# A fused attention and MoE kernel: another order of its loads, with one batch's transposes and one block's sums done in another way

## The chip, the cores and the metric

The kernel runs on one core of a Trainium2 chip. The metric is the device time of one execution in microseconds (us), the median of 10 runs: 512.66 us before the change, all runs between 512.37 and 512.99.

A core has five engines with a queue of instructions each: TensorE (PE) for matmuls and transposes, VectorE (DVE) and ScalarE (ACT) for elementwise work, GpSimd (POOL) and SyncE (SP), which here issue DMAs. [...]Loads are issued by POOL[...]; stores and DMA transposes are issued by SP. An engine runs its queue in order, so an instruction that waits holds up everything behind it.

## The reference

Linformer attention for 8 batches of 8 heads, 1024 positions, head size 64, with keys and values projected to 64 rows; then an MLP with a sigmoid GELU over all 8192 tokens.

```python
k_proj = np.einsum('ks,bhsd->bhkd', E, k)
v_proj = np.einsum('ks,bhsd->bhkd', F, v)
scores = np.matmul(q, k_proj.transpose(0, 1, 3, 2)) / sqrt(64)
attn = softmax(scores)
x = matmul(attn, v_proj)      # (8, 8, 1024, 64) -> tokens x 512
h = x @ w_in                  # 512 -> 2048
g = h * (1.0 / (1.0 + np.exp(-1.702 * h)))
out = g @ w_out               # 2048 -> 512
```

The softmax's maximum is not subtracted by the kernel; the scores are small.

## The kernel before

**Blocks.** The 8192 tokens are cut into 16 blocks `j` of 512; a batch `b` is two blocks, `h = 2b` and `2b + 1`. A block's MLP is 16 calls of `ffn1` (slots 0 to 15, each four matmuls of 128x512 and a GELU on ACT), then `ffn2`, eight parts of eight matmuls (slots `O` = 16 onward; two parts for each of four output tiles of 128 tokens). Block 0 is cut smaller, since its inputs are still arriving: its `ffn1` runs in halves of 256 tokens (slots 0 to 31), and its `ffn2` slots are counted from `Q` = 32.

**Attention between the MLP's slots.** The attention of later blocks is put between the slots by hand: `at(j, slot, f)` files `f`, and `filled(j, slot)` runs it after that slot. TensorE's order is thus fixed by this list. For a batch: `proj(b)` projects `k` and `v` (16 matmuls in pairs, key rows in the lower and value rows in the upper half of PSUM's partitions); `kv_out(b)` copies them out on DVE and, from batch 2 on, transposes `k` by a DMA on SP's queue into `kts[b % 2]`; for batch 1 `k_tr` does it with four TensorE transposes. `q_dma(b)` transposes `q` on SP's queue into `qT[b]`. For a block: `scores(h, u)` for `u` = 0, 1 makes the scores of four heads by two groups of eight small matmuls (`eight`, L262) and their exponentials on ACT (L278).

**Three ways to normalize.** Blocks 0 to 2 use `tok` and `x_tr`: the values with a column of ones, tokens on the partitions, a division, and a transpose back. Block 3 uses `norm`: the sums of the exponentials by eight matmuls with ones, spread over all partitions at once, then DVE's reciprocal of the full 128x512 tile four times. Blocks from 4 on use `sums` (eight matmuls of one row each, two reciprocals), `spread` (the reciprocals are written to DRAM and read back, repeated over 64 partitions, as `rbc`) and `values` (matmuls, then one DVE multiplication by `rbc`).

**PSUM.** `f_tile` takes a bank from the pool `ps_f`, which `ffn1`, `ffn2`, `proj` and the scores share; `x_ps` tiles come from `ps_x`, used by `tok`, `x_tr`, `sums`, `norm`, `values`.

**Loads.** `k_sb`, `v_sb` and `q_sb` are one buffer each (`ldpool` has `bufs=1`), and batch 0's `q` has its own, `q0_sb`. A load waits until the batch ahead has been read. POOL's order at the start is: `k` of batch 0, its `q` in the first two of eight column groups `j`, `v`, the next two `j`, six of eight parts of `w_in`, the second half of `q` in one DMA (Block 1's `q`), two parts of `w_in`, four parts of `w_out`, then `load(1)`: `k`, `v`, `q`. `load(b)` for `b` > 1 is `k`, `q`, `v`. A batch's `q` is eight DMAs of 128 KB, in which each head's row of 64 numbers is a run of its own; `k` and `v` are 1 MB each in longer runs. (Sizes are those in bfloat16.) Each load on POOL's queue also waits for the load eight places ahead of it[...].

**Block 1's `q`** is transposed by TensorE (`q_tr(2)`, `q_tr(3)`, L244, 32 transposes) in slots 20 and 23 of block 0.

**The end.** The last of the 64 output tiles is cut into two halves of 256 columns (L397): ACT copies one, DVE the other (L399), each with its own store.

Of the kernel before, what the change touches and what calls it, by code (L numbers as in the profile page):

```python
# [9 lines left out]
F32 = mybir.dt.float32  # L10
# [7 lines left out]
def kernel(ctx, tc, q, k, v, E, F,  # L18
# [37 lines left out]
        for h, n in [(h, hs) for h in range(0, H, hs)] if isinstance(hs, int) else hs:  # L56
            nc.gpsimd.dma_start(out=dst[b][:, h:h + n, js:js + jn], in_=sv[:, h:h + n, js:js + jn])  # L57

    def load_q(b):
        qt[b] = ldpool.tile([P, J, H, D], BF16, name="q_sb")  # L60
        qv = q[b].rearrange("h (p j) d -> p j h d", p=P)
        for j in range(J):
            nc.gpsimd.dma_start(out=qt[b][:, j], in_=qv[:, j])  # L63

    def load(b):
        load_kv(k, kt, b, "k_sb")
        if b == 1:
            load_kv(v, vt, b, "v_sb")
        load_q(b)
        if b > 1:  # L70
            load_kv(v, vt, b, "v_sb")

    w_in_v = moe_w_in.rearrange("(c p) f -> p c f", p=P)
    w_out_v = moe_w_out.rearrange("(c p) m -> p c m", p=P)
# [8 lines left out]
    load_kv(k, kt, 0, "k_sb", ((0, 4), (4, 2), (6, 2)))  # L83
    ident = consts.tile([P, P], BF16)
    make_identity(nc, ident)
    load_kv(q, qt, 0, "q0_sb", H, 0, 2)
    load_kv(v, vt, 0, "v_sb", ((0, 4), (4, 2), (6, 2)))
    load_kv(q, qt, 0, "q0_sb", H, 2, 2)
    for i in range(6):
        load_w_in(i)  # L90
    load_kv(q, qt, 0, "q0_sb", H, JB, JB)
    for i in range(6, 8):
        load_w_in(i)
    for i in range(4):
        sl = slice(i * FC // 4, (i + 1) * FC // 4)
        nc.gpsimd.dma_start(out=w_out_sb[:, sl, :], in_=w_out_v[:, sl, :])
    load(1)
# [31 lines left out]
    def f_tile(shape, dt=F32):  # L129
        return ps_f.tile(shape, dt, name="f_ps")  # L130
# [24 lines left out]
        return efts[j // (J // 2)][:, j % (J // 2), cols]  # L155


    kvps, kbs, qT, expT, xT, rbc, rdens = {}, {}, {}, {}, {}, {}, {}

    def proj(b):  # L160
        def go():
# [15 lines left out]
    def k_piece(h0, n):  # L177
        k_ps = proj0(0, h0, n)
        k_b = att.tile([KP, n, D], BF16, name=f"k0_b{h0}", bufs=1)
        nc.vector.tensor_copy(k_b, k_ps[LO])  # L180
        warm(2)
        k_tr(0, k_b, h0 // 2)

    def k_tr(b, k_b, p0):
        n = k_b.shape[1] // 2
        t_ps = f_tile([P, n, KP], BF16)
        for p in range(n):
            nc.tensor.transpose(t_ps[:, p, :], k_b[:, 2 * p:2 * p + 2, :].rearrange("k t d -> k (t d)"),
                                ident[:KP, :KP])
        nc.vector.tensor_copy(kts[b % 2][:, p0:p0 + n, :], t_ps)  # L190

    def vx_of(b, p):
        if b == 1:
# [21 lines left out]
    def kv_out(b):  # L215
        def go():
            ps = kvps.pop(b)
            k_b = att.tile([KP, H, D], BF16, name="k_b")
            nc.vector.tensor_copy(k_b, ps[LO])  # L219
            if b > 1:  # L220
                nc.sync.dma_start_transpose(out=kts[b % 2], in_=k_b.rearrange("k h d -> k (h d)"))
            v_out(b, ps)
            kbs[b] = k_b
        return go

    q0s = [[consts.tile([P, 2, 2, P], BF16, name=f"q0T{g}{u}") for u in range(2)] for g in range(2)]
# [1 line left out]
    def q_tr0(g, u, cp):  # L228
        t_ps = f_tile([P, 2, 2, P], BF16)
        for jj in range(2):  # L230
            for h in range(4):
                r = h % 2 * D
                nc.tensor.transpose(t_ps[r:r + D, jj, h // 2, :], qt[0][:, 4 * u + h, 2 * g + jj, :], ident)  # L233
        cp(q0s[g][u], t_ps)

    def q_tr(g):
        def go():
            if 0 not in qT:
                qT[0] = att.tile([P, J, HP, P], BF16, name="qT")
            t_ps = f_tile([P, 2, HP, P], BF16)  # L240
            for jj in range(2):
                for h in range(H):
                    r = h % 2 * D
                    nc.tensor.transpose(t_ps[r:r + D, jj, h // 2, :], qt[0][:, h, 2 * g + jj, :], ident)  # L244
            nc.vector.tensor_copy(qT[0][:, 2 * g:2 * g + 2], t_ps)
        return go

    def q_dma(b, j0=0, n=J):
        def go():
            if j0 == 0:  # L250
                qT[b] = att.tile([P, J, HP, P], BF16, name="qT")
            nc.sync.dma_start_transpose(out=qT[b][:, j0:j0 + n].rearrange("r j p s -> r (j p) s"),
                                        in_=qt[b][:, j0:j0 + n].rearrange("s j h d -> s (j h d)"))
        return go
# [10 lines left out]
    def scores(h, u, half=None):  # L265
        b, c = divmod(h, NB2)
        j0, n = (c * JB, JB) if half is None else (c * JB + half * JB // 2, JB // 2)
        ts = slice(j0 * P - c * TB, (j0 + n) * P - c * TB)

        def go():  # L270
            if h not in expT:
                expT[h] = att.tile([P, HP, TB], BF16, name="expT", bufs=3)
            s_ps = [f_tile([P, n * P]) for _ in range(2)]
            eight(s_ps, [kts[b % 2][:, 2 * u + i, :] for i in range(2)],
                 [q0s[half][u][:, :, i, :] if h == 0 else qT[b][:, j0:j0 + n, 2 * u + i, :]
                   for i in range(2)])
            for i in range(2):
                nc.scalar.activation(expT[h][:, 2 * u + i, ts], s_ps[i], AF.Exp, scale=scale)  # L278
        return go
# [105 lines left out]
    def ffn2(j, n, fcs):  # L385
        b, c = divmod(j, NB2)
        ov = out[b * S:(b + 1) * S, :].rearrange("(p j) m -> p j m", j=J)
        if j not in osb:
            osb[j] = work.tile([P, JB, DM], F32, name="o_sb")
        if j == NBLK - 1 and n == JB - 1:  # L390

            if fcs.start == 0:
                for i, cp in enumerate((nc.scalar.copy, nc.vector.tensor_copy)):
                    ms = slice(i * DM // 2, (i + 1) * DM // 2)
                    l_ps = f_tile([P, DM // 2])
                    for fc in range(FC):
# [49 lines left out]
    q_tr0(1, 1, DV)  # L446

    order = [(half, fc) for fcs in (range(12), range(12, FC)) for half in range(2) for fc in fcs]
    at(0, 0, scores(0, 0, 1))
    at(0, 1, scores(0, 1, 1), gelu_table)  # L450
    for p in range(HP):
        at(0, 2 + p, tok(0, p, 1))
        at(0, 5 + p, x_tr(0, p, 1))
    at(0, 20, q_tr(2))
    at(0, 23, q_tr(3))
    for u in range(2):
        at(0, Q + u, scores(1, u))
    at(0, Q + 1, gelu_table)
    for p in range(HP):
        at(0, Q + (2, 4, 6, 7)[p], tok(1, p, 0), tok(1, p, 1))  # L460
        at(0, Q + (4, 6, 7, 8)[p], x_tr(1, p, 0), x_tr(1, p, 1))
    at(1, 10, proj(1))
    at(1, 11, kv_out(1))
    at(1, 13, lambda: k_tr(1, kbs[1], 0))
    at(1, 1, q_dma(1, 0, JB), q_dma(1, JB, JB))
    for u in range(2):
        at(1, O + u, scores(2, u))
        at(1, O + 3 + u, scores(3, u))
        at(2, O + 2 * u, scores(4, u))
    for p in range(HP):  # L470
        at(1, O + 2 + p, tok(2, p, 0), tok(2, p, 1))
        at(1, O + 3 + p, x_tr(2, p, 0), x_tr(2, p, 1))
    at(1, O + 5, gelu_table)
    at(1, O + 4, q_dma(2))
    at(2, 0, proj(2), kv_out(2))
    at(2, 1, norm(3, 0))
    at(2, 11, norm(3, 1))
    at(2, O, q_dma(3))
    at(2, O + 4, scores(5, 0))
    at(2, O + 6, proj(3), kv_out(3), scores(5, 1), sums(4), spread(4))  # L480
    at(2, O + 7, gelu_table)
    for b in range(4, B):
# [23 lines left out]
    for j in range(NBLK):  # L506
        if j % NB2 == 0 and j // NB2 + 2 < B:
            load(j // NB2 + 2)
        for i, (half, fc) in enumerate(order if j == 0 else [(None, fc) for fc in range(FC)]):
            ffn1(j, fc, slice(0, TB) if half is None else slice(half * TB // 2, (half + 1) * TB // 2))  # L510
            filled(j, i)
        parts = [(n, range(8 * g, 8 * g + 8)) for n in range(JB) for g in range(2)]
        if j == 0:
            parts[:4] = [(n, fcs) for fcs in (range(8), range(8, 12), range(12, FC)) for n in range(2)]
        for s, (n, fcs) in enumerate(parts):
            ffn2(j, n, fcs)
            filled(j, (Q if j == 0 else O) + s)
# [31 lines left out]
```

## Time and profile before

| What | us |
|---|---|
| median of 10 runs | 512.66 |
| the profiled execution | 512.86 |
| its span in the profile | 511.1 |
| first `ffn1` matmul (block 0) | 21.16 |
| first `ffn2` matmul (block 0) | 38.35 |
| first `ffn1` matmul of block 1 | 54.86 |
| `proj(1)` starts | 64.45 |
| `scores(2, 0)` | 72.77 |
| `proj(2)`, first `v` matmul | 90.21 |
| `proj(3)` starts | 119.83 |
| one ordinary block, with and without a `proj` (`ffn1` at 184.53, 213.69, 244.71) | 31.0, 29.2 |
| last matmul group of 256 columns begins (chain of waits) | 504.38 |

How to read the profile: "PE" is TensorE's matmuls, "PEld" its weight loads, which run beside them; "L373" is line 373 of the kernel. A group's row gives the output and input tiles, the shape, how many there were, then the busy time, the mean duration in ns, and the idle time of the engine just before, with what ended it. A matmul's duration is longer than its distance from the next one, since matmuls overlap: 512-column matmuls follow each other every 0.216 us (eight of them in 1.73 us). The DMA view counts packets, MB and the share of the 16 transfer engines for POOL's loads ("software_dynamic") and for what SP issues ("hardware_dynamic").

The engines' rows by stage, where the first number is the time, then the busy time and number of instructions of each engine, the granted TensorE clock, the DMA share and GB/s:

```profile
21.00:38.00 17.00, 17.00 (x198) 14.21 (x194) 6.50 (x20) 13.35 (x36) 7.97 (x11) 1.00 1.37 201
38.00:55.00 17.00, 16.84 (x115) 8.53 (x117) 6.15 (x24) 7.32 (x12) 4.18 (x5) 1.00 1.45 197
55.00:71.00 16.00, 15.95 (x85) 7.04 (x84) 2.51 (x6) 9.54 (x16) 4.08 (x5) 1.00 1.32 186
71.00:88.00 17.00, 16.90 (x126) 8.02 (x127) 6.15 (x24) 9.07 (x14) 4.66 (x6) 1.00 1.80 173
88.00:106.00 18.00, 17.40 (x112) 7.36 (x113) 12.80 (x8) 9.29 (x16) 7.85 (x9) 1.00 1.24 195
```

### The profile page before, as it was taken

The numbers are of one execution on the slowest core, as the hardware profiler recorded it, in microseconds if no ns is written. First come the engines' busy times: TensorE is split into PE (matmuls) and PEld (weight loads), VectorE is DVE, ScalarE is ACT, GpSimd is POOL, SyncE is SP. The second block draws the span as 40 slices with busy tenths as digits, with TensorE's granted clock in tenths as the row PEclk, the third lists the DMA queues.
The fourth block names the chain that finished last, engine by engine and source line by source line (L and its number), as shares of the span: only waits on it lengthen the run. The fifth ranks groups of instructions, "written<-read, shape, count | busy, mean of one in ns | idle before, by whom it ended". The sixth has DMA issues, their size and how long they took to land.

```text
span 511.1 us, 7183 instructions
## 1 busy us (share of the span) xinstructions
PE 499.7 (98%) x3039; PEld 232.0 (45%) x3090; DVE 164.9 (32%) x221; ACT 264.1 (52%) x443; POOL 78.0 (15%) x97
## 2 busy tenths in 40 slices
PE   8999999999999999999999999999999999999997
PEld 4684444444444444444444444444444444444444
DVE  4523114764161622316151341615214161611000
ACT  1675564554637356471746637374563737244351
POOL 7542051514200051000510033000000000000000
PEclk9999999999999999999999999999999999999999
DMA  9999999999989089751997249990603205050202
GB/s 165 197 203 207 214 143 161 219 179 138 165 240 218 1 173 195 149 151 38 213 165 199 54 93 211 118 246 1 171 1 69 98 6 160 1 166 1 82 1 82
DMA packets 124752, 67.64 MB, mean 132 GB/s; under 512 B 92288, under 2 KB 116096, under 8 KB 122800
## 3 DMA queue, kind: packets, MB, share of 16 engines
q0 software_dynamic: 84400, 29.37, 51.6%
q1 hardware_dynamic: 40240, 37.56, 29.0%
q8 instruction: 24, 0.39, 0.3%
q10 hardware_dynamic: 80, 0.26, 0.3%
q14 instruction: 8, 0.07, 0.1%
HBM read 71.83 MB, written 16.97 MB: 174 GB/s over the span
## 4 chain that ended last, share of the span: by engine, by line
PE 85%; DMA 10%; issue 4%; ACT 0%; DVE 0%; POOL 0%; ACTq 0%; POOLq 0%
PE f_ps L373 39%; PE f_ps L405 37%; DMA v_sb<-in_v_dram 7%; PE f_ps L165 2%; DMA k_sb<-in_k_dram 2%; PE f_ps L262 2%; PE x_ps L262 1%; DMA ef_f<-in_E_dram 1%; PE x_ps L135 1%; PE f_ps L173 1%; PE x_ps L297 1%; PE f_ps L397 0%; POOL q_sb L63 0%; PE f_ps L233 0%; PE x_ps L359 0%
## 5 line engine op out<-in xcount | busy, mean ns | idle before, releaser
L373 PE MATMUL f_ps<-xT,w_in_sb 128*128 128x512 bf16 (+1 forms) x1071 | 225.3, 366 | 0.9
L405 PE MATMUL f_ps<-w_out_sb,gT 128*128 128x512 bf16 x976 | 221.4, 379 | 4.0 <-issue 3.5
L376 ACT ACTIVATE gT<-f_ps 128x512 bf16<-128x512 f32 (+1 forms) x270 | 151.8, 574 | 61.8 <-PE f_ps L373 60.5
L373 PEld LDWEIGHTS <-w_in_sb 128*128 128x128 bf16 x1088 | 105.4, 98 | 115.5 <-issue 1.7
L405 PEld LDWEIGHTS <-gT 128*128 128x128 bf16 x1008 | 95.5, 98 | 120.5 <-issue 11.3
L408 ACT COPY o_sb<-f_ps 128x512 f32<-128x512 f32 x63 | 36.9, 586 | 126.8 <-PE f_ps L405 117.1
L332 DVE TENSOR_TENSOR xT<-x_ps,rbc 128x512 bf16<-128x512 f32 x48 | 30.9, 686 | 201.3 <-PE x_ps L262 124.8
L300 DVE RECIPROCAL rden<-x_ps 128x512 f32<-128x512 f32 x24 | 78.7, 3322 | 10.3 <-PE x_ps L297 10.3
L63 POOL DMA_DIRECT2D q_sb<-in_q_dram x56 | 49.1, 900 | 55.5 <-DMA k_sb<-in_k_dram 41.8
L278 ACT ACTIVATE expT<-f_ps 128x512 bf16<-128x512 f32 (+1 forms) x68 | 35.1, 572 | 32.7 <-PE f_ps L262 32.7
L57 POOL DMA_DIRECT2D k_sb<-in_k_dram x10 | 8.4, 844 | 173.5 <-PE f_ps L165 156.7
L219 DVE CAST k_b<-f_ps 64x512 bf16<-64x512 f32 x7 | 4.8, 683 | 47.7 <-PE f_ps L165 47.7
L278 ACT ACT_TABLE_LOAD x13 | 16.7, 1283 | 4.7 <-PE f_ps L262 4.5
L282 ACT ACT_TABLE_LOAD x14 | 18.0, 1283 | 0.2
L165 PE MATMUL f_ps<-v_sb,eft 128*64 128x512 bf16 x56 | 13.4, 381 | 0.5 <-DMA v_sb<-in_v_dram 0.5
L322 DVE RECIPROCAL rdn<-x_ps 128x512 f32<-128x512 f32 x4 | 13.4, 3352 | 0.8 <-PE x_ps L262 0.8
L165 PE MATMUL f_ps<-k_sb,eft 128*64 128x512 bf16 x56 | 13.6, 382 | 0.0
L399 DVE COPY o_sb<-f_ps 128x256 f32<-128x256 f32 x1 | 0.4, 424 | 38.6 <-issue 38.6
L135 PE MATMUL x_ps<-zeros 128*128 128x512 bf16 x32 | 11.4, 474 | 1.3 <-DVE zeros L106 1.2
L262 PE MATMUL f_ps<-qT,kt 64*32 64x512 bf16 x240 | 12.3, 387 | 0.0
L262 PE MATMUL x_ps<-expT,vq 64*32 64x512 bf16 x208 | 10.2, 377 | 0.0
L262 PEld LDWEIGHTS <-kt 64*32 64x32 bf16 x272 | 3.9, 88 | 13.7 <-issue 13.5
(71 smaller groups left out, 127.7 us busy)
## 6 DMA issues: line engine op xcount, KB each, us to landing
out_dram<-o_sb SPq DMA_DIRECT2D x15, 1024.0 KB
rbc<-rdr SPq DMA_DIRECT2D x24, 512.0 KB
k_sb<-in_k_dram POOLq DMA_DIRECT2D x7, 1024.0 KB, 14.5
v_sb<-in_v_dram POOLq DMA_DIRECT2D x7, 1024.0 KB, 10.5
q_sb<-in_q_dram POOLq DMA_DIRECT2D x56, 128.0 KB, 11.9
w_in_sb<-in_moe_w_in_dram POOLq DMA_DIRECT2D x8, 256.0 KB, 11.8
w_out_sb<-in_moe_w_out_dram POOLq DMA_DIRECT2D x4, 512.0 KB, 14.7
out_dram<-o_sb SPq DMA_DIRECT2D x3, 256.0 KB
```

What stands on the lines that cost most here:

```text
L63: nc.gpsimd.dma_start(out=qt[b][:, j], in_=qv[:, j])
L135: nc.tensor.matmul(w_ps, zeros[:, :P], zeros, start=True, stop=True)
L165: nc.tensor.matmul(kvps[b][r], eft(j, slice(e * KP, (e + 1) * KP)), (kt, vt)[e][b][:, :, j, :], start=(j == 0), stop=(j == J - 1))
L262: nc.tensor.matmul(outs[i][r.start + c:r.start + c + 32], lhsTs[i][ri, c:c + 32], rhss[i][ri], start=True, stop=True)
L278: nc.scalar.activation(expT[h][:, 2 * u + i, ts], s_ps[i], AF.Exp, scale=scale)
L282: nc.scalar.preload_act_table(AF.Gelu_apprx_sigmoid)
L300: nc.vector.reciprocal(rden[:, e, :], d_ps[e])
L332: nc.vector.tensor_tensor(x_of(h)[:, 2 * u + i, :], n_ps[i], rbc[h][:, 2 * u + i, :], op=ALU.mult)
L373: nc.tensor.matmul(h_ps, w_in_sb[:, kc, fc * P:(fc + 1) * P], xT[j][:, kc, ts], start=(kc == 0), stop=(kc == KC - 1))
L376: nc.scalar.activation(gts[j][:, fc, ts], h_ps, AF.Gelu_apprx_sigmoid)
L405: nc.tensor.matmul(o_ps[n], gts[j][:, fc, n * P:(n + 1) * P], w_out_sb[:, fc, :], start=(fc == 0), stop=(fc == FC - 1))
L408: nc.scalar.copy(osb[j][:, n, :], o_ps.pop(n))
```

## The change

1. Loads at the start: Block 1's `q` is now loaded by four DMAs of one column group each, between parts 2 and 3 of `w_out`; all eight parts of `w_in` come ahead of it. Batch 0's `q` shares its buffer `q_even` with batch 2's; all other batches use `q_sb`.
2. Order within a batch: batches 1 and 2 `k`, `q`, `v`; batch 3 `k`, `v`, `q`; from batch 4 on `q`, `k`, `v`. With one `q_sb`, a `q` load waits for the DMA transposes of the batch ahead.
3. Block 1's `q` and batch 1's `k` are transposed by DMAs on SP's queue, no longer by TensorE (`q_tr` goes, `k_tr` stays for batch 0).
4. Block 3 uses `sums`, `spread` and `values` in place of `norm`.
5. Scores of both `u` are put at one slot, one of them (or both) in banks of `ps_x`; block 0's `scores(1)` moves from the first two slots of `ffn2` to slot `Q + 7`, and the `tok` and `x_tr` behind it too. `proj(1)` and `proj(2)` move one slot later.
6. Block 0's `ffn2` runs in quarter parts (four matmuls), over three output tiles side by side, then the fourth.
7. The last output tile is cut into 256, 128 and 128 columns.

```diff
+    def q_buf(b):
+        return ldpool.tile([P, J, H, D], BF16, name="q_even" if b in (0, 2) else "q_sb")
+
+    def load_q(b, j0=0):
+        if j0 == 0:
+            qt[b] = q_buf(b)
         qv = q[b].rearrange("h (p j) d -> p j h d", p=P)
-        for j in range(J):
+        for j in range(j0, J):
             nc.gpsimd.dma_start(out=qt[b][:, j], in_=qv[:, j])
 
+    def load_q0(j0, n):
+        nc.gpsimd.dma_start(out=q0_sb[:, :, j0:j0 + n],
+                            in_=q[0].rearrange("h (p j) d -> p h j d", p=P)[:, :, j0:j0 + n])
+
     def load(b):
-        load_kv(k, kt, b, "k_sb")
-        if b == 1:
-            load_kv(v, vt, b, "v_sb")
-        load_q(b)
-        if b > 1:
-            load_kv(v, vt, b, "v_sb")
+        for what in ("kqv", "kqv", "kvq", "qkv")[min(b, 4) - 1]:
...
-    load_kv(q, qt, 0, "q0_sb", H, 2, 2)
-    for i in range(6):
-        load_w_in(i)
-    load_kv(q, qt, 0, "q0_sb", H, JB, JB)
-    for i in range(6, 8):
+    load_q0(2, 2)
+    for i in range(8):
         load_w_in(i)
     for i in range(4):
+        if i == 2:
+            load_q(0, JB)
         sl = slice(i * FC // 4, (i + 1) * FC // 4)
         nc.gpsimd.dma_start(out=w_out_sb[:, sl, :], in_=w_out_v[:, sl, :])
...
-            if b > 1:
-                nc.sync.dma_start_transpose(out=kts[b % 2], in_=k_b.rearrange("k h d -> k (h d)"))
+            nc.sync.dma_start_transpose(out=kts[b % 2], in_=k_b.rearrange("k h d -> k (h d)"))
             v_out(b, ps)
-            kbs[b] = k_b
...
-            s_ps = [f_tile([P, n * P]) for _ in range(2)]
+            s_ps = [(x_tile() if x else f_tile([P, TB]))[:, :n * P] for _ in range(2)]
...
-                for i, cp in enumerate((nc.scalar.copy, nc.vector.tensor_copy)):
-                    ms = slice(i * DM // 2, (i + 1) * DM // 2)
-                    l_ps = f_tile([P, DM // 2])
+                for m0, m, cp in ((0, 2, nc.vector.tensor_copy), (2, 1, nc.vector.tensor_copy), (3, 1, nc.scalar.copy)):
+                    ms = slice(m0 * DM // 4, (m0 + m) * DM // 4)
+                    l_ps = f_tile([P, m * DM // 4])
...
-    at(0, 0, scores(0, 0, 1))
-    at(0, 1, scores(0, 1, 1), gelu_table)
+    at(0, 1, scores(0, 0, 1), scores(0, 1, 1, True), gelu_table)
...
-    at(0, 20, q_tr(2))
-    at(0, 23, q_tr(3))
+    at(0, 20, q_dma(0, JB, JB))
     for u in range(2):
-        at(0, Q + u, scores(1, u))
-    at(0, Q + 1, gelu_table)
+        at(0, Q + 7, scores(1, u, None, True))
+    at(0, Q + 8, gelu_table)
     for p in range(HP):
-        at(0, Q + (2, 4, 6, 7)[p], tok(1, p, 0), tok(1, p, 1))
-        at(0, Q + (4, 6, 7, 8)[p], x_tr(1, p, 0), x_tr(1, p, 1))
-    at(1, 10, proj(1))
-    at(1, 11, kv_out(1))
-    at(1, 13, lambda: k_tr(1, kbs[1], 0))
+        at(0, Q + 9 + p, tok(1, p, 0), tok(1, p, 1))
+        at(0, Q + 11 + p, x_tr(1, p, 0), x_tr(1, p, 1))
     at(1, 1, q_dma(1, 0, JB), q_dma(1, JB, JB))
+    at(1, 11, proj(1), kv_out(1))
     for u in range(2):
-        at(1, O + u, scores(2, u))
-        at(1, O + 3 + u, scores(3, u))
-        at(2, O + 2 * u, scores(4, u))
+        at(1, O, scores(2, u, None, u > 0))
+        at(2, O, scores(4, u, None, u > 0))
+        at(2, O + 3 * u, values(3, u))
...
-    at(1, O + 5, gelu_table)
+    for u in range(2):
+        at(1, O + 6, scores(3, u, None, u > 0))
+    at(1, O + 6, gelu_table)
     at(1, O + 4, q_dma(2))
-    at(2, 0, proj(2), kv_out(2))
-    at(2, 1, norm(3, 0))
-    at(2, 11, norm(3, 1))
+    at(2, 1, proj(2), kv_out(2), sums(3), spread(3))
     at(2, O, q_dma(3))
-    at(2, O + 4, scores(5, 0))
+    at(2, O + 3, scores(5, 0))
...
-            parts[:4] = [(n, fcs) for fcs in (range(8), range(8, 12), range(12, FC)) for n in range(2)]
+            parts = [(n, range(4 * g, 4 * g + 4)) for ns in (range(3), (3,)) for g in range(4) for n in ns]
```

The waits of the built program follow: SP's transpose of Block 1's `q` waits for the four DMAs that bring it, and `scores(1)` for that transpose; batch 1's `v` load waits for the first of batch 1's eight `q` loads; SP's queue holds, in this order, the transpose of Block 1's `q`, the store of block 0, two transposes of batch 1's `q`, the transpose of its `k`, the transpose of batch 2's `q`.

More of the change, by code (lines that the diff above doesn't have):

```diff
@@ L57, in load_kv @@
             nc.gpsimd.dma_start(out=dst[b][:, h:h + n, js:js + jn], in_=sv[:, h:h + n, js:js + jn])
-    def load_q(b):
-        qt[b] = ldpool.tile([P, J, H, D], BF16, name="q_sb")
+    def q_buf(b):
[3 more added lines that the diff above has]
+            qt[b] = q_buf(b)
         qv = q[b].rearrange("h (p j) d -> p j h d", p=P)
-        for j in range(J):
+        for j in range(j0, J):
             nc.gpsimd.dma_start(out=qt[b][:, j], in_=qv[:, j])
+    def load_q0(j0, n):
+        nc.gpsimd.dma_start(out=q0_sb[:, :, j0:j0 + n],
+                            in_=q[0].rearrange("h (p j) d -> p h j d", p=P)[:, :, j0:j0 + n])
     def load(b):
-        load_kv(k, kt, b, "k_sb")
-        if b == 1:
-            load_kv(v, vt, b, "v_sb")
-        load_q(b)
-        if b > 1:
-            load_kv(v, vt, b, "v_sb")
+        for what in ("kqv", "kqv", "kvq", "qkv")[min(b, 4) - 1]:
+            if what == "q":
+                load_q(b)
+            elif what == "k":
+                load_kv(k, kt, b, "k_sb")
+            else:
+                load_kv(v, vt, b, "v_sb")
     w_in_v = moe_w_in.rearrange("(c p) f -> p c f", p=P)
@@ L85 @@
     make_identity(nc, ident)
-    load_kv(q, qt, 0, "q0_sb", H, 0, 2)
+    qt[0] = q_buf(0)
+    q0_sb = qt[0][:, :JB].rearrange("p j h d -> p (j h d)").rearrange("p (h j d) -> p h j d", h=H, j=JB)
+    load_q0(0, 2)
     load_kv(v, vt, 0, "v_sb", ((0, 4), (4, 2), (6, 2)))
-    load_kv(q, qt, 0, "q0_sb", H, 2, 2)
-    for i in range(6):
-        load_w_in(i)
-    load_kv(q, qt, 0, "q0_sb", H, JB, JB)
-    for i in range(6, 8):
+    load_q0(2, 2)
+    for i in range(8):
         load_w_in(i)
     for i in range(4):
+        if i == 2:
+            load_q(0, JB)
         sl = slice(i * FC // 4, (i + 1) * FC // 4)
@@ L155, in eft @@
         return efts[j // (J // 2)][:, j % (J // 2), cols]
-    kvps, kbs, qT, expT, xT, rbc, rdens = {}, {}, {}, {}, {}, {}, {}
+    kvps, qT, expT, xT, rbc, rdens = {}, {}, {}, {}, {}, {}
     def proj(b):
@@ L181, in k_piece, with k_tr @@
         warm(2)
-        k_tr(0, k_b, h0 // 2)
-    def k_tr(b, k_b, p0):
+        k_tr(k_b, h0 // 2)
+    def k_tr(k_b, p0):
         n = k_b.shape[1] // 2
@@ L189, in k_tr @@
                                 ident[:KP, :KP])
-        nc.vector.tensor_copy(kts[b % 2][:, p0:p0 + n, :], t_ps)
+        nc.vector.tensor_copy(kts[0][:, p0:p0 + n, :], t_ps)
     def vx_of(b, p):
@@ L232, in q_tr0 @@
                 r = h % 2 * D
-                nc.tensor.transpose(t_ps[r:r + D, jj, h // 2, :], qt[0][:, 4 * u + h, 2 * g + jj, :], ident)
+                nc.tensor.transpose(t_ps[r:r + D, jj, h // 2, :], q0_sb[:, 4 * u + h, 2 * g + jj, :], ident)
         cp(q0s[g][u], t_ps)
[L236 to L246, printed above, removed]
     def q_dma(b, j0=0, n=J):
         def go():
-            if j0 == 0:
+            if b not in qT:
                 qT[b] = att.tile([P, J, HP, P], BF16, name="qT")
@@ L263, in eight, with x_tile, scores @@
                                      start=True, stop=True)
-    def scores(h, u, half=None):
+    def x_tile():
+        return ps_x.tile([P, TB], F32, name="x_ps")
+    def scores(h, u, half=None, x=False):
         b, c = divmod(h, NB2)
```

## The prediction

> **What bounds the kernel now.** I read the page's busy times first, then the chain of work that ended last.
>
> ```profile
> PE 499.7 (98%) x3039; PEld 232.0 (45%) x3090; DVE 164.9 (32%) x221; ACT 264.1 (52%) x443; POOL 78.0 (15%) x97
> PE 85%; DMA 10%; issue 4%; ACT 0%; DVE 0%; POOL 0%; ACTq 0%; POOLq 0%
> ```
>
> TensorE is busy 499.7 of 511.1 us; the rest is the wait for the first inputs and the last store. So time is saved only by taking instructions off TensorE, and lost only by making it wait. The 10% of DMA in the chain are not idle time of TensorE: its waits list has a single DMA, 0.5 us, for `v` of batch 2. The page's slices show the transfer engines full from the start to about 120 us. The question is thus where in the first four blocks TensorE comes near a transfer. The timelines of TensorE and of POOL's queue answer it for batch 1:
>
> ```profile
> 54.86 9.66 PE L373 MATMUL f_ps<-xT,w_in_sb 128*128 128x512 bf16 x44
> 64.45 0.40 PE L165 MATMUL f_ps<-k_sb,eft 128*64 128x512 bf16 x1
> ...
> 48.38 0.88 POOL L63 DMA_DIRECT2D q_sb<-in_q_dram  x1 [4.22 <-DMA k_sb<-in_k_dram]
> 53.41 0.87 POOL L63 DMA_DIRECT2D q_sb<-in_q_dram  x1 [4.16 <-DMA v_sb<-in_v_dram]
> ```
>
> Every load from the ninth on waits for the load eight places ahead, so these two issues date landings: `k` of batch 1 at 48.2 us, `v` at 53.1 us, and `proj(1)`, which needs both, starts at 64.45. `v` has 11.3 us to spare. The last `q` load, issued at 53.41, lands after 7.1 us, at 60.5.
>
> Then the transfers in half-microsecond windows, from 56.0 (`q` alone), 59.0 (the store of block 0 beside it), 87.0, 87.5 and 88.5 (the transposes of `q` of batch 2 beside the end of `v`) and 91.0 (those transposes alone); columns are packets, MB and share of the engines:
>
> ```profile
> q0 software_dynamic: 613, 0.08, 242.3%
> ...
> q1 hardware_dynamic: 20, 0.16, 77.7%
> q0 software_dynamic: 82, 0.01, 40.5%
> ...
> q1 hardware_dynamic: 214, 0.05, 110.0%
> q0 software_dynamic: 63, 0.06, 68.6%
> ...
> q1 hardware_dynamic: 195, 0.05, 410.8%
> q0 software_dynamic: 22, 0.02, 25.1%
> ...
> q1 hardware_dynamic: 34, 0.01, 19.6%
> q0 software_dynamic: 10, 0.01, 11.3%
> ...
> q1 hardware_dynamic: 568, 0.15, 127.8%
> ```
>
> The loads (software queue) give way to SP's stores and transposes (hardware queue): to 82 packets from 613 beside a store, to about half the bytes beside transposes, and about 2.3 us nearly stood still (87.5 to 89.8). `v` of batch 2 landed only at 90.17, and that is the 0.5 us wait.
>
> [...]here 568 packets of 256 B in 0.5 us are 290, and I use that. [...]the granted clock is 1.00 in every window[...].
>
> **The change, part by part**, in times of this execution (512.86 us, span 511.1; 0.2 above the median of 512.66).
>
> *TensorE work that goes.* The 32 transposes of Block 1's `q` (L244): two gaps of 0.57 us in the timeline (32.29 to 32.86, 34.28 to 34.85), 1.14 us. `k_tr(1)` (68.99 to 69.21): 0.22. Scores whose two halves are put together: a lone group of eight matmuls costs 0.34 us, two in a row 0.56, so 0.12 for each of four pairs (blocks 1 to 4), and about 0.2 for block 0's (0.23 + 0.40 against 0.44): 0.68. Block 3: `norm` costs 0.55 twice; `sums` beside other small matmuls 0.22, `values` 0.22 twice: 0.44 saved. Sum 2.48 us. DVE's four reciprocals of 3.35 us become two; DVE is off the path.
>
> *Block 1's `q`.* It was one 512 KB load behind six parts of `w_in`. Now it is four of 128 KB between w_out's parts 2 and 3, with runs of 256 B in place of 1 KB, and a transpose on SP's queue takes TensorE's place. By the windows runs of 256 B move 0.154 MB in 1 us, larger ones 0.205, so 0.5 MB take 3.4 us, not 2.56: +0.85. From `w_in` part 5, landed at 27.5: two parts of `w_in` (1.25 each), two of w_out (2.5 each), `q` 3.4, so it lands near 38.5. SP issues the transpose, which takes 1.5 to 3 us until the first packet (85.04 to 86.6, 111.98 to 115.0) and 2,048 packets at 214 to 290 per half microsecond, 4.2 us in the middle, with a standstill (2.3) or none: done at 44.7 to 48.5. TensorE wants it for `scores(1)` after eight quarter parts: 38.35 - 1.14 - 0.2 + 8 x 0.86 = 43.9. First new wait, 1 to 4.6 us, I take 2.5. Behind it stand all of TensorE's later work, and the store of block 0 on ACT's copies.
>
> *Batch 1: `k`, `q`, `v`.* Now `v` is the last of everything in the first stream. Pure load work before it ends where `q`'s ended, 60.5, less 1.6 that the store took from it (1,495 packets in 2.8 us from 57.5 where 3,433 fit), plus 0.85: 59.7. To that come hardware transfers that fall ahead of it: Block 1's `q` transpose 1.8 (0.5 MB at 290 GB/s); the store 2.8; of batch 1's `q` transposes, which start when `q` lands and now run beside `v`, between 0.9 (packet for packet) and 3.1 (3.4 to 1), I take 2.7; one standstill 2.3 (none 0, two 4.6). 59.7 + 1.8 + 2.8 + 2.7 + 2.3 = 69.3 us. `proj(1)`, one slot later, would be reached at 64.45 - 1.14 - 0.2 - 0.12 + 0.86 = 63.85. So TensorE waits 5.45 us in all, of which the first wait is a part, not an addition: what it loses at `scores(1)` it doesn't lose again at `proj(1)`. The bounds: 59.7 + 1.8 + 2.8 + 0.9 = 65.2 gives 1.4, two standstills give about 7.7.
>
> *`kt(1)` by DMA transpose.* From the end of `proj(1)`: cast 0.7, then as for batch 3 (issued 122.53, packets over at 124.5) 3 us; `scores(2)` comes 4 x 0.86 + 1.73 = 5.2 us after `proj(1)`. Hidden by 1.5 us; behind unfinished transposes, up to 1.5 late. I take 0.
>
> *Batch 2.* Load 2 still starts at the end of `proj(1)`; from there to `v` it took 24 us, and TensorE needs it after 23.2 - 0.46 + 0.86 = 23.6. The 0.5 us wait stays about as it is; 0, or a gain of 0.5.
>
> *Block 3 by `sums`, `spread`, `values`.* In batch 3's like stage the reciprocals ended at 130.0 and `rbc` had landed by 147.8. From the end of `proj(2)`, 8.2 + 17.8 = 26 us; `values(3,0)` holds two PSUM buffers until then, and the next to need them, `sums(4)`, comes after 27.7. Hidden by about 0.3 us, and more as `k` and `v` are read first; 0, at worst 2.
>
> *`v` of batch 3 ahead, `q` first from batch 4.* `q` of batch 3 landed at 111.9 and its scores come at 138; `v` landed at 116.9 and was used at 119.8. Later batches have whole blocks to spare: batch 5's `k` issued at 182.44, its last load at 198.97, its `proj` at 240.4. That each `q` load waits for the transpose ahead stops only POOL, whose queue holds nothing but loads. 0.
>
> *The last tile in three.* The final copy is half as wide (0.31 for 0.42 us, by the shorter ACT copies) and the store too, but 128-column matmuls take 0.069 us (L173's) where half of the 256 column ones is 0.055: about 0.3 back. 0, within 0.4.
>
> *Sum.* 512.86 - 2.48 + 5.45 = 515.8; on the median's scale 515.6. Nothing smaller than 0.2% (1.0 us) can be told from no change.
>
> **Rivals.**
> 1. The transfers don't collide: `v` lands by 64 us, because loads keep their rate while SP's packets fill gaps. For it speaks that the share of the engines beside transposes passes 100%, so there is overlap; against it the 613 that became 82. It gives 512.66 - 2.48 = 510.2; it decides once `v` lands before about 65 us (wait under 1.5). Chance 0.20.
> 2. Waits of about 2.5 us in all cancel the saving: 512.7. Lower bounds everywhere. Chance 0.08.
> 3. Everything late: two standstills, a late `kt(1)`, [...]late `rbc`. [...]half of it gives 518 to 519. Chance 0.17.
> 4. The change doesn't do what it says: `q` first makes `k` and `v` of each later batch late. Three batches with a wait of 1 us would be 518. The slack of tens of us speaks against it. Chance 0.03.
>
> **How the numbers follow.** My forecast, a slower kernel by TensorE's wait for `v` of batch 1, has 0.52, with its own range of 513.8 to 518. Faster is rival 1, 0.20; within 0.2% is rival 2 and the edges of the others, 0.08; slower 0.72. The range that holds 8 in 10 takes half of rival 1 and of rival 3: 510.2 to 519.5.
>
> **What would show it.** Right: a TensorE wait of several us at `proj`'s first `v` matmul in block 1, put down to `v_sb`; one at block 1's first scores, put down to the transpose; no L244; `v` landing at 68 to 71 us; blocks 5 to 16 unchanged at 29.2 and 31.0 us. Wrong: no DMA wait on TensorE before 75 us (rival 1), or a wait in a later block (rival 4).

## The result, and the profile after

The median is 523.57 us (8 runs, 522.86 to 526.45) against 512.67 for the kernel before on the same chip (29 runs). The ratio is 1.0224, interval 1.0213 to 1.0234: slower by 10.9 us. The profiled execution took 525.55 us, 12.69 more than the profiled one of before and 2.0 above its own median. The account below is in profiled times; kernels are compared by medians.

The page of the changed kernel, busy times and the chain that ended last:

```profile
PE 499.1 (95%) x3011; PEld 232.2 (44%) x3062; DVE 156.4 (30%) x217; ACT 263.7 (50%) x443; POOL 80.6 (15%) x100
...
PE 87%; DMA 10%; issue 1%; POOL 1%; DVE 0%; ACT 0%; SPq 0%; POOLq 0%
```

TensorE is busy as long as before, though work was taken off it, and the span grew from 511.1 to 523.8. The list of waits (waiter, releaser: us in all, how often, the longest) has two new DMAs on TensorE, and no `v_sb` any more. The first line is from the kernel before, the others from the changed one:

```profile
PE f_ps L165 <- DMA v_sb<-in_v_dram: 0.5, 1, 0.5
...
PE x_ps L260 <- DMA qT<-q_even: 9.8, 1, 9.8
...
PE f_ps L260 <- DMA kt<-k_b: 2.5, 1, 2.5
```

TensorE's timeline places them (start, us, what, count, idle time before it and its releaser):

```profile
37.35 7.07 PE L406 MATMUL f_ps<-w_out_sb,gT 128*128 128x512 bf16 x31
54.24 1.05 PE L260 MATMUL x_ps<-qT,kt 64*32 64x512 bf16 x16 [9.82 <-DMA qT<-q_even]
...
66.07 10.52 PE L374 MATMUL f_ps<-xT,w_in_sb 128*128 128x512 bf16 x47
76.52 0.40 PE L177 MATMUL f_ps<-k_sb,eft 128*64 128x512 bf16 x1
...
86.26 0.63 PE L260 MATMUL f_ps<-qT,kt 64*32 64x512 bf16 x8 [2.54 <-DMA kt<-k_b]
```

The first is `scores(1)`, which has to have Block 1's transposed `q`; the second is `scores(2)`, which has to have `kt(1)`. What stood behind `scores(1)` in TensorE's queue stood still with it: TensorE was busy 0.42 of the 6 us from 44 to 50. Between the two `proj(1)` starts at 76.52 without a wait. The chain dates the transfers (start, us):

```profile
27.97 10.95 DMA q_even<-in_q_dram
...
39.01 15.19 DMA qT<-q_even
...
79.22 7.00 DMA kt<-k_b
```

`q` landed at 38.9, and its transpose then took 15.19 us from issue to landing: its first packets came at 42.5, its last at 53.5. Why is seen in the transfers of single half microseconds. Here are, in order, those from 44.0, 46.5, 50.5, 80.5 and 85.0 (packets, MB, share of the engines):

```profile
q0 software_dynamic: 76, 0.08, 91.2%
q1 hardware_dynamic: 78, 0.02, 30.2%
...
q1 hardware_dynamic: 9, 0.00, 39.0%
q0 software_dynamic: 5, 0.01, 12.8%
...
q1 hardware_dynamic: 112, 0.03, 115.3%
q0 software_dynamic: 110, 0.02, 82.6%
...
q0 software_dynamic: 18, 0.02, 73.7%
q1 hardware_dynamic: 239, 0.06, 70.7%
...
q0 software_dynamic: 87, 0.09, 120.8%
q1 hardware_dynamic: 14, 0.00, 3.9%
```

At 44.0 the transpose (q1) and the load stream (q0) go packet for packet, 78 to 76. A packet of the transpose carries 256 B and one of the load 1 KB, so the transpose gets a fifth of the bytes: 0.02 MB where it moves 0.15 alone. At 46.5 both nearly stand still, for half a microsecond. From 49 on the load's packets are mostly the small ones of batch 1's `q`, of 128 B in the trace. Both queues then get more packets through (175 and 178 at 49.5), and at 50.5 too, where the load's packets are no larger than the transpose's, it is one for one. The last two windows belong to `kt(1)`: at 80.5 its data go through, 239 packets; at 85.0 14 more are still arriving, of 4 B each in the trace. Over the windows from 84.5 there are 32 of these (12, 14, 6), and only after the last is the transpose done, at 86.22.

A third part of the loss is in no list of waits. The windows of the same trace (stretch, its length, busy time of PE, PEld, DVE, ACT and POOL, granted clock, DMA share, GB/s):

```profile
44.00:50.00 6.00, 0.42 (x2) 0.00 (x0) 0.00 (x0) 0.00 (x0) 0.87 (x1) 0.89 1.30 172
...
56.00:58.00 2.00, 1.78 (x5) 0.76 (x5) 0.00 (x0) 1.98 (x3) 0.00 (x0) 0.50 3.57 146
58.00:60.00 2.00, 2.00 (x13) 1.06 (x12) 0.85 (x4) 0.86 (x2) 0.00 (x0) 0.77 2.51 162
...
86.00:88.00 2.00, 1.40 (x17) 0.44 (x19) 0.00 (x0) 1.07 (x3) 0.05 (x1) 0.55 1.31 143
88.00:90.00 2.00, 2.00 (x7) 0.78 (x6) 0.00 (x0) 1.00 (x3) 0.00 (x0) 0.59 2.10 143
90.00:92.00 2.00, 2.00 (x13) 0.94 (x12) 0.00 (x0) 0.58 (x1) 1.63 (x2) 1.00 2.42 154
```

After both waits TensorE works at half its clock, and takes about twice as long: four matmuls of 512 columns took 1.91 us from 56.91 and 1.03 from 58.99. The clock falls at about 48.7 (0.89 over 44 to 50), within the first wait, and stays down until about 58.9 (0.77 over 58 to 60), 4.7 us after work came back, then again from the end of the second wait until about 89.6 (0.59 over 88 to 90), 3.4 us after. Half of that is lost: 2.3 and 1.7 us. This is at least part of why PE is nearly as busy as before with less to do: the 4.0 us were spent busy.

The sum in profiled times: 9.82 + 2.3 + 2.54 + 1.7 = 16.4 lost, 2.48 saved by the prediction's own count, and the 0.5 us wait for `v` of batch 2 gone: +13.4, where +12.69 was measured. The mean granted clock is on record for every run: 0.986 in the profiled one, 0.984 in the slowest (526.45), 0.990 in all the others. The step from 0.986 to 0.990 is some 2 us less lost to the slow clock, which is about what the profiled execution lies above the median. From block 5 on the blocks take 29.2 and 31.0 us, as before.

### The profile page after: what moved, and what is told of

Same layout as the page of the kernel before. It is cut to its first block, busy times and chain, and to the rows that moved or that the text cites. A ratio compares the mean times of both kernels' runs of the same rounds, so it can differ in the third digit from the quotient of the medians.

```text
span 523.8 us, 7133 instructions
## 1 busy us (share of the span) xinstructions
PE 499.1 (95%) x3011; PEld 232.2 (44%) x3062; DVE 156.4 (30%) x217; ACT 263.7 (50%) x443; POOL 80.6 (15%) x100
## 4 chain that ended last, share of the span: by engine, by line
PE 87%; DMA 10%; issue 1%; POOL 1%; DVE 0%; ACT 0%; SPq 0%; POOLq 0%
PE f_ps L406 40%; PE f_ps L374 39%; DMA qT<-q_even 3%; PE f_ps L177 2%; DMA w_in_sb<-in_moe_w_in_dram 2%; DMA q_even<-in_q_dram 2%; DMA v_sb<-in_v_dram 2%; PE f_ps L260 2%; PE x_ps L260 2%; DMA kt<-k_b 1%; PE f_ps L398 1%; PE x_ps L298 1%; POOL k_sb L57 0%; PE x_ps L345 0%; PE x_ps L360 0%
## 5 line engine op out<-in xcount | busy, mean ns | idle before, releaser
L333 DVE TENSOR_TENSOR xT<-x_ps,rbc 128x512 bf16<-128x512 f32 x52 | 33.3, 684 | 219.0 <-PE x_ps L260 118.1
L301 DVE RECIPROCAL rden<-x_ps 128x512 f32<-128x512 f32 x26 | 85.3, 3322 | 10.3 <-PE x_ps L298 10.2
L69 POOL DMA_DIRECT2D q_sb<-in_q_dram x48 | 42.0, 909 | 153.4 <-DMA qT<-q_sb 133.5
L279 ACT ACTIVATE expT<-f_ps 128x512 bf16<-128x512 f32 (+1 forms) x56 | 29.0, 572 | 32.4 <-PE f_ps L260 32.3
L350 DVE RECIPROCAL rd<-x_ps 128x4 f32<-128x4 f32 x22 | 3.8, 174 | 43.3 <-PE x_ps L345 43.3
L279 ACT ACTIVATE expT<-x_ps 128x512 bf16<-128x512 f32 (+1 forms) x12 | 6.0, 576 | 15.7 <-PE x_ps L260 15.7
L177 PE MATMUL f_ps<-k_sb,eft 128*64 128x512 bf16 x56 | 13.4, 382 | 0.0
L177 PE MATMUL f_ps<-v_sb,eft 128*64 128x512 bf16 x56 | 13.4, 382 | 0.0
L260 PE MATMUL f_ps<-qT,kt 64*32 64x512 bf16 x200 | 10.5, 395 | 2.5 <-DMA kt<-k_b 2.5
L260 PE MATMUL x_ps<-qT,kt 64*32 64x512 bf16 x40 | 2.5, 523 | 9.8 <-DMA qT<-q_even 9.8
## 6 DMA issues: line engine op xcount, KB each, us to landing
k_sb<-in_k_dram POOLq DMA_DIRECT2D x7, 1024.0 KB, 13.7
```

The source lines that it names most:

```text
L177: nc.tensor.matmul(kvps[b][r], eft(j, slice(e * KP, (e + 1) * KP)), (kt, vt)[e][b][:, :, j, :], start=(j == 0), stop=(j == J - 1))
L301: nc.vector.reciprocal(rden[:, e, :], d_ps[e])
L333: nc.vector.tensor_tensor(x_of(h)[:, 2 * u + i, :], n_ps[i], rbc[h][:, 2 * u + i, :], op=ALU.mult)
```

## The experiments

The theory after the result (A): the two DMA transposes are slow because they share the transfer engines packet for packet with a load stream of larger packets; TensorE waits for them; everything else in the change is small. Rivals (B, of two kinds): the wait would be found somewhere else once these are gone (`v` of batch 1, as predicted), or such transposes are slow whatever stands beside them. The letters in the expectations below are each run's own.

| kernel | median us (runs) | ratio to before, interval |
|---|---|---|
| after | 523.57 (8) | 1.0224, 1.0213 to 1.0234 |
| e1: `q` by TensorE | 514.96 (6) | 1.0043, 1.0030 to 1.0057 |
| e2: `k` by TensorE | 522.67 (4) | 1.0196, 1.0179 to 1.0213 |
| e3: both | 511.95 (14) | 0.9988, 0.9979 to 0.9996 |
| e4: both, and `k`, `v`, `q` in batch 1 | 511.87 (14) | 0.9984, 0.9974 to 0.9994 |
| e5: `q` loaded earlier | 519.86 (4) | 1.0147, 1.0116 to 1.0177 |
| e6: loads held back for `q` | 529.27 (4) | 1.0327, 1.0290 to 1.0364 |
| e7: e3 without the new order of batches 3 to 7 | 519.37 (5) | 1.0126, 1.0108 to 1.0144 |
| e8: before, with block 3's sums | 514.05 (19) | 1.0039, 1.0021 to 1.0056 |
| e9: e8, and `v` of batch 3 ahead of `q` | 512.41 (13) | 0.9999, 0.9991 to 1.0007 |
| e10: e1, load of batch 2 held back for `kt(1)` | 516.60 (4) | 1.0086, 1.0070 to 1.0101 |

### One transpose at a time given back to TensorE (e1, e2, e3)

```diff
-    at(0, 20, q_dma(0, JB, JB))
+    at(0, Q + 4, q_tr(2))
+    at(0, Q + 5, q_tr(3))
```

`q_tr` is the function of before, 16 transposes and a copy each, with its tiles in the other PSUM pool; the diff leaves it out.

> The changed kernel, but Block 1's q is transposed by TensorE again (32 transposes after the fifth and sixth quarter parts of block 0), from the same late load. Theory A (the DMA transpose of Block 1's q advances packet for packet with the loads, 70 packets to 77 in half a microsecond, and TensorE waits for it): the 9.8 us wait goes, and with it the 2.3 us that the halved clock cost, for 1.1 us of transposes: 523.6 - 11 = 512.5, with the wait for kt(1) still there. Theory B (the forecast's: batch 1's v behind q is the real limit, and only hidden by the first wait): a wait for v_sb of 2 to 6 us appears at proj(1), and the time is 515 to 519. Theory C (the place of the q load between w_out's parts, not its transpose): TensorE now waits at L244-like transposes for q itself, and little is won.

e1 took 514.96: 8.6 of the 10.9 us come back, less than the 11 expected. No DMA wait is left at `scores(1)` and none is at `proj(1)`. The list of waits still has one, longer than the 2.5 us of before this edit:

```profile
PE f_ps L272 <- DMA kt<-k_b: 3.6, 1, 3.6
```

The price of the slow clock can be read here between runs of one kernel: five of the six runs have a mean clock of 0.996 and took 514.78 to 515.68, the sixth has 1.000 and took 513.15 (how long its wait was is not recorded).

```diff
-            nc.sync.dma_start_transpose(out=kts[b % 2], in_=k_b.rearrange("k h d -> k (h d)"))
+            if b > 1:
+                nc.sync.dma_start_transpose(out=kts[b % 2], in_=k_b.rearrange("k h d -> k (h d)"))
...
+    at(1, 13, lambda: k_tr(kbs[1], 0, 1))
```

> The changed kernel, but batch 1's k is transposed by TensorE (four transposes, two slots after proj(1)) and not by SP's queue. If the DMA transpose's 7 us from issue to landing are what scores(2) waits for, the 2.5 us wait and the 1.7 us of halved clock behind it go for 0.2 us of transposes: 4.0 us less, 519.6. If scores(2) would wait anyway (for q's transposes), the time stays at 523 or more.

e2 keeps the first wait, and the one for `kt` is gone:

```profile
PE x_ps L263 <- DMA qT<-q_even: 9.8, 1, 9.8
```

Its median is only 0.9 us below that of after, where 4.0 were expected, while the profiled executions differ by 3.2 (525.55 to 522.36). The clocks account for most of that: all runs of after but the profiled one and the slowest have 0.990, as the profiled one of e2 has. Most runs of after thus lost some 2 us less to the slow clock than the profiled one; how long their second wait was is not recorded.

> The changed kernel with both transposes given back to TensorE: Block 1's q and batch 1's k. If these two DMA transposes are all that the change lost, no DMA wait is left on TensorE, the clock is 1.00, and the time is that of the kernel before less the savings that remain (scores in pairs 0.7, block 3's sums 0.4, batch 2's wait for v 0.5 to 0.9): 511.0. If v behind q in batch 1 (the forecast's mechanism) bites once both are gone, proj(1) waits for v_sb and the time is 512 to 516.

e3 has both edits, and is below the kernel before: by 0.12%, at most 0.21 by its interval, which is at the edge of what can be told. With `kt` alone still on DMA (e1) the median was 3.0 higher; with `q` alone (e2), 10.7. No wait took the place of the two, as the first B had it: the waits for transfers in its profile are 1.7 us for batch 0's `k` at the start, ahead of everything that the edits touch, 0.3 for `v` of batch 2 and 0.2 for `w_in`. The pairs of scores, the order of `ffn2` and the cut of the last tile were not run alone; what they do together is within this result.

### `v` ahead of `q` in batch 1 again (e4)

```diff
-        for what in ("kqv", "kqv", "kvq", "qkv")[min(b, 4) - 1]:
+        for what in ("kvq", "kqv", "kvq", "qkv")[min(b, 4) - 1]:
```

> As the run with both transposes on TensorE, and batch 1's v is loaded ahead of its q. If v behind q costs nothing there, the same time within 0.3 us. If it costs something, this one is faster by that. A loss is possible too: q of batch 1 then lands later, its transposes meet load(2), and scores(2) waits for them.

511.87 against 511.95: no difference that can be told, and these two are the best versions here. The wait that the prediction had at the centre, for `v` of batch 1, costs nothing once the transposes are off the queue. (The profile of e4 has the 1.7 us at the start too, and 1.1 for `v` of batch 2.)

### The transfer of `q` against the load stream (e5, e6)

```diff
     for i in range(8):
+        if i == 6:
+            load_q(0, JB)
         load_w_in(i)
     for i in range(4):
-        if i == 2:
-            load_q(0, JB)
```

> The changed kernel, but Block 1's q is loaded ahead of w_in's last two parts, as before the change, still by four DMAs and still transposed by a DMA on SP's queue. Theory A: the transpose still takes 13 to 16 us from issue to landing, because the loads still run beside it; it is issued near 31.5 us instead of 39.0, lands near 46, and TensorE waits some 2 us at scores(1) instead of 9.8: about 515. The forecast's reading (3.4 packets of the transpose to one of the loads): 6 us, no wait, 511 to 513. Theory C: no wait either, since q lands 7 us earlier.

The transpose was issued at 31.86 instead of 39.01, and its packets ran from 35.5 to 50, at about 78 to 78 in each half microsecond but for a near standstill at 48.5: some 14 us for 2,048 packets, and 18.66 from issue to landing. It had 7 us more, and TensorE still waited:

```profile
PE x_ps L260 <- DMA qT<-q_even: 5.4, 1, 5.4
PE f_ps L260 <- DMA kt<-k_b: 2.2, 1, 2.2
```

That is more than the 2 us that A expected, and 519.86 is more than its 515: started earlier, the transpose meets the load's large packets from its first packet to its last, and takes longer (18.66 against 15.19).

```diff
+    q_tap = consts.tile([P, 8], BF16, name="q_tap")
...
+    nc.sync.dma_start_transpose(out=qT[0][:, JB:].rearrange("r j p s -> r (j p) s"),
+                                in_=qt[0][:, JB:].rearrange("s j h d -> s (j h d)"))
+    nc.gpsimd.tensor_copy(q_tap, qT[0][:, J - 1, HP - 1, :8])
     load(1)
...
-    at(0, 20, q_dma(0, JB, JB))
```

> The changed kernel, but POOL copies eight numbers out of Block 1's transposed q before it issues load(1), so that beside the transpose there are only w_out's last two parts (1,024 packets) and nothing after them. Theory A: the first half of the transpose's 2,048 packets goes one for one with those loads, the second half alone at 0.5 us for each 568; from first to last packet 5 to 7 us instead of 10.5, landing near 49, and the first wait is about 4 us or less. If the transpose is slow by itself or by its standstill, it takes 10 us or more from first to last packet as in the changed kernel. The loads of batch 1 start later by 12 us or so, so a wait for v_sb comes at proj(1) in any case, and the total says little: 518 to 524.

The copy on POOL makes the load of batch 1 wait until the transposed `q` is there. The half microseconds from 43.5 and 44.0 of its trace, where no load is under way:

```profile
q1 hardware_dynamic: 472, 0.12, 113.3%
...
q1 hardware_dynamic: 567, 0.15, 128.0%
```

The same 2,048 packets took 3.5 us (41.5 to 45.0), the first 2 of these beside the last 200 or so packets of a load, and `scores(1)` waited 2.9 us. So the transpose is not slow whatever stands beside it, as the second B had it. But the loads, begun that much later, were missed at `proj(1)`, by 13.0 us, and the kernel is slower than the 518 to 524 expected. The quick transpose was had at the loads' expense.

### The last packets of `kt(1)` (e10)

```diff
+            if b == 1:
+                nc.gpsimd.tensor_copy(k_tap, kts[1][:, HP - 1, :8])
+                load(2)
             v_out(b, ps)
...
-            load(j // NB2 + 2)
+            if j > 0:
+                load(j // NB2 + 2)
```

The edits of e1 stand beside these. The last three lines take `load(2)` out of its old place, the start of block 0's loop.

> e1 with the load of batch 2 held back on POOL until the transposed k of batch 1 has landed (a small copy that reads it). Theory A (the last packets of that transpose are late because the load starts at the same moment): issue to landing falls from 8.1 to about 3 us, the wait for kt at scores(2) goes (under 0.5), and the load of batch 2, 3 us later, gives a wait for v_sb of about 4 at proj(2); 514 to 516 in all. Theory B (such a small transpose takes 7 to 8 us whatever stands beside it): the wait for kt stays at 3.6 and the v_sb wait of about 5 comes on top, some 520.

The transpose was issued at 68.29, as in e1 (68.20), and POOL's copy that reads its result ran at 70.61: landed within 2.3 us, where e1 shows 8.06. First the half microseconds from 69.5 and 70.0 of e10:

```profile
q1 hardware_dynamic: 244, 0.06, 68.4%
...
q1 hardware_dynamic: 32, 0.00, 2.9%
```

and those from 69.5, 73.5 and 74.0 of e1:

```profile
q1 hardware_dynamic: 233, 0.06, 71.5%
q0 software_dynamic: 25, 0.03, 33.4%
...
q0 software_dynamic: 94, 0.10, 124.5%
q1 hardware_dynamic: 15, 0.00, 4.2%
...
q0 software_dynamic: 81, 0.08, 113.0%
q1 hardware_dynamic: 10, 0.00, 2.8%
```

The data move at the same moment in both. The last 32 packets follow at once where nothing loads, and come 4 us later, between 73 and 76 (15 and 10 of them in the windows shown), where the load of batch 2 has begun. That load is issued 0.17 us before the transpose, by the end of the same `proj(1)`. So it is the load beside it, not the transpose, that makes 8 us of 2.3. In e10 the wait went to `v` of batch 2 in its place (3.9 us at `proj(2)`), and the kernel is slower than e1.

### The order of batch 3, and block 3's sums (e7, e8, e9)

```diff
-        for what in ("kqv", "kqv", "kvq", "qkv")[min(b, 4) - 1]:
+        for what in ("kqv", "kqv", "kqv", "kqv")[min(b, 4) - 1]:
```

> As the run with both transposes on TensorE, but with batches 3 to 7 loaded in the order k, q, v, as before the change. The forecast took the new order (v ahead in batch 3, q first from batch 4) at nothing: the same time within 0.3 us. If q first helps or harms the later batches, a difference of 0.5 us or more, spread over the blocks from 3 on.

e7 is 7.4 us slower than e3. Its profile has one long wait, 5.9 us at `proj(3)` (the other 0.2 are at `proj(2)`):

```profile
PE f_ps L178 <- DMA v_sb<-in_v_dram: 6.1, 2, 5.9
```

It ends at 124.8, and the clock is at half until about 128.3, which is another 1.7 us. `v`, issued at 108.46, is now the last load of batch 3. Ahead of it the read-back of block 3's reciprocals (`rbc`, 1 MB, issued from 106.62) runs beside the last of batch 3's `q` loads (the last is issued at 107.26). What such a read-back does to loads of `q` can be read in the profile of after: they moved 0.16 MB in the microsecond from 123, and 0.01 to 0.02 in each from 125 to 128, beside its `rbc` (0.19 to 0.22). So the order of before costs 7.4 us in this kernel. That the sums are the reason, by putting `rbc` there, was not tried in it (no run has the old order with `norm`), but on the kernel before:

```diff
+        at(2, O + 3 * u, values(3, u))
...
-    at(2, 0, proj(2), kv_out(2))
-    at(2, 1, norm(3, 0))
-    at(2, 11, norm(3, 1))
+    at(2, 1, proj(2), kv_out(2), sums(3), spread(3))
```

> The kernel before with one part of the change alone: block 3's sums in one round, spread through DRAM, in place of norm, with proj(2) one slot later. The forecast has 0.44 us less TensorE work and up to 0.5 us less wait for v of batch 2: 511.8 to 512.2. If rbc lands too late for sums(4) (the rival cost, at worst 2 us), 513 or more.

514.05, with runs from 512.91 to 520.63: slower by 0.4%, and less steady than before on the same chip (512.74, with runs from 512.12 to 515.26). Its profiled execution was a good one (513.24). Even there `v` of batch 3 was issued at 105.56, just ahead of `rbc` (106.52), and TensorE waited 0.3 us for `v` at a `proj`; that the longer runs had a later `v` is inferred, not seen. One more edit tests it:

```diff
-        if b == 1:
+        if b in (1, 3):
             load_kv(v, vt, b, "v_sb")
         load_q(b)
-        if b > 1:
+        if b not in (1, 3):
```

> The kernel before with two parts of the change alone: block 3's sums (as in e8) and v of batch 3 loaded ahead of its q. Theory A (in e8 v of batch 3 arrives beside the read-back of block 3's reciprocals, some runs late; ahead of q it is over before): 511.7 to 512.2, with a narrow spread, and no v_sb wait at proj(3). Theory B (e8's spread comes from something else): as e8, about 514 with runs up to 520.

512.41, between 512.08 and 513.74: 1.6 us below e8, and its profile has no wait for a transfer at any `proj`. It ran on another chip than e8, where before too was steadier (512.54, with runs from 512.23 to 513.15), so the two are best compared by their ratios to before, 0.9999 and 1.0039. Against before e9 is neither faster nor slower. The sums with their order of loads are thus worth nothing measurable; without it they cost 0.4% there.

## Why the prediction was right or wrong

The sign was right, and so were the place of the first wait (`scores(1)`, for the transposed `q`) and `q`'s landing ("near 38.5"; 38.9). The size of that wait was wrong, and with it the total. The sign is in part luck: it came from 5.45 us of waiting for `v` of batch 1, which did not happen. With the 2.5 us taken for the first wait alone, the prediction's sum would have been 512.9, no change.

- **The step that failed: "2,048 packets at 214 to 290 per half microsecond, 4.2 us in the middle, with a standstill (2.3) or none: done at 44.7 to 48.5".** Done at 54.20. The packets ran for 11 us, from 42.5 to 53.5: until 49 at 62 to 86 per half microsecond beside the load's 1 KB packets, but for half a microsecond of standstill, then faster beside small ones. e5, beside large packets throughout, shows 78; only nearly alone does the same transpose take 3.5 us (e6). The wait is 9.8 us, where "1 to 4.6 us, I take 2.5" stood. The 214 to 63 came from the end of a load: from 87.0 on in the kernel before, 123 of the 1,024 packets of `v` were left. The 82 beside the store came from one too, with 134 left from 59.0 on. The other end of the range is a slip: 290 is the transpose's GB/s alone, and in packets that is the 568 per half microsecond of the prediction's own line. It made the forecast slower, toward what came. Where both queues are full the windows show one for one: 78 to 76, 112 to 110. The same prediction used "packet for packet" as a lower bound for batch 1's `q`; here, at the 78 per half microsecond of the trace, it gives 2,048 / 78 x 0.5 = 13 us.
- **`v` of batch 1 at "69.3 us", and so a wait of "5.45 us in all".** The last packets of the loads before `proj(1)` came at about 64.7. Of the terms, the store (2.8) and batch 1's transposes (2.7) fell away: since TensorE was late, SP issued them at 66.88 and 67.41, behind `v`. From 59.7 to 64.7 leaves 5.0 for the first transpose and its standstill, where 4.1 was taken. With `proj(1)` reached at 76.52 nothing was waited for there, and e4 shows that `v` last costs nothing without the transposes either (e1: `proj(1)` at 65.5 without a wait). In e1 the store and batch 1's transposes do run ahead of the end of `v`, issued at 55.86 and 56.40, and its last packets still come by 63.5, ahead of that `proj(1)`.
- **`kt(1)`: "Hidden by 1.5 us", "I take 0".** 2.54 us, and 1.7 by the clock behind it; in e1 3.6. The duration was taken from `kt(3)` of before, "packets over at 124.5". Those were its data: 32 packets follow there at 127.5 to 129.5, as here. Issue to landing is 7.0 us, not 3.
- **The clock.** Rival 3 had a term for it, an estimate of the author's that no trace of before shows (the granted clock was 1.00 in its windows). The forecast's sum had it at nothing. In the profiled execution it was at half after both waits, and 4.0 us were lost together.
- **Order of loads from batch 3 on, "0".** Right against before only as a pair: e9 gives 0.9999 for sums and order together, while the order alone is worth 7.4 us once the sums are there (e7). Block 3's step, "Hidden by about 0.3 us", missed that `rbc` competes with the loads. (Its terms, 26 us against 27.7, leave 1.7, not 0.3.)
- **"Sum 2.48 us" of TensorE work.** Not measured by itself. e3 gives back 1.14 and 0.22 of it, which leaves 1.12; its median is 0.8 below that of before on the same chip (512.74), by the ratio 0.6.
- Rival 4 (later batches) was rightly small: no wait for a transfer after 90 us in the profile after. Of the terms of rival 3, everything late, the late `kt(1)` and the halved clock came; two standstills and a late `rbc` at `sums(4)` did not.

## What to carry to other kernels

In these runs a DMA transpose was cheap only where the transfer engines were free (2,048 packets in 3.5 us in e6, in about 14 beside a load in e5). Beside a running load stream, price it by counting its packets one for one with the load's (78 to 76 in half a microsecond here), and expect it to complete some 4 to 5 us later when a load is issued at the same moment (seen for transposes of 64 KB: 7.0 and 8.06 us from issue to landing, against 2.3). Take a ratio between two queues only from windows where both have work left. A wait of TensorE for a transfer of 2.2 us or more cost another 1.4 to 2.9 us in the profiles here (half of the time at half clock after work came back), so where a few transposes on TensorE (1.14 us here) avoid one, they are the cheaper way.

## What the runs showed of the hardware that was not expected

- Where both had work left, as many packets of a load went through as of a transpose, with load packets of 1 KB (78 to 76 in half a microsecond of after, 78 to 78 in e5) and with mostly 128 B (112 to 110); 2,048 packets of 256 B took 3.5 us nearly alone and about 14 beside 1 KB packets. The read-back of `rbc` went one for one with loads too: 91 to 91 in the microsecond from 143 of before (0.18 MB to 0.09), 103 to 101 in that from 128 of after (0.21 MB to 0.01).
- A transpose of 64 KB counted as landed only after 32 packets more, of 4 B each, which came at once without a load beside them and 4 to 5 us late with one (2.3 against 8.06 us from issue to landing).
- The granted clock fell to 0.50 around waits of TensorE for a transfer, the shortest of them 2.18 us. In the profiles waits of 2.18 (e5), 2.54 (after), 2.93 (e6), 3.60 (e1) and 3.88 us (e10) were all followed by half clock for some 2.8 to 3.4 us; waits of 0.5 (before), 1.0 (e6), 1.1 (e4) and 1.7 us (e3) were not. The stretches at half clock have few lengths: about 3.4 us (the second ones of after and e5, e1, e10), 6.8 (e7), 10.2 (the first of after), 13.7 (e6, around its wait of 13.0). Windows of e5 around its wait of 2.18, which ended at 82.75:

```profile
82.00:83.00 1.00, 0.25 (x15) 0.14 (x16) 0.00 (x0) 0.00 (x0) 0.58 (x1) 1.00 1.23 205
84.00:86.00 2.00, 2.00 (x6) 0.64 (x5) 0.00 (x0) 1.26 (x3) 0.00 (x0) 0.50 2.13 144
86.00:87.00 1.00, 1.00 (x4) 0.44 (x3) 0.00 (x0) 0.32 (x1) 0.76 (x1) 0.50 2.43 155
87.00:88.00 1.00, 1.00 (x6) 0.41 (x5) 0.00 (x0) 0.26 (x1) 0.68 (x2) 0.98 2.43 155
```

Here the clock was still full when work came back, fell at some point of the microsecond left out (0.81 over 83 to 84), and returned at 87. Why the clock fell around these waits, and not around those of 1.7 us and less, the runs do not settle.
